# A lone tile computed with its tokens stationary and the weights moving, in a fused attention and mixture-of-experts kernel on one core

## The chip, the cores and the metric

The kernel runs on one core of a Trainium2 chip. The metric is the device time of one execution in microseconds (us), the median of the runs.

## What is computed

Per batch and head, keys and values are averaged over groups of 8, and softmax attention runs against the 72 averaged keys. The result, 4608 rows of 512, is routed: each row goes to the one of 8 experts with the largest gate, through `relu(x @ w1[e]) @ w2[e]`, and is scaled by two gate factors.

```python
x = attn_out.transpose(0, 2, 1, 3).reshape(B * S, H * D)     # 4608 x 512
e_idx = np.argmax(x @ w_gate, axis=1)
for e in range(E):
    mask = e_idx == e
    h = np.maximum(x[mask] @ w1[e], 0.0)                      # 512 -> 1024
    ye = h @ w2[e]                                            # 1024 -> 512
    out[mask] = gate_w[mask, None] * eom[mask, e, None] * ye
```

With the inputs of seed 0 the experts get 1018, 55, 333, 239, 827, 724, 24 and 1388 rows: 8, 1, 3, 2, 7, 6, 1 and 11 tiles of 128. Experts 1 and 6 have one tile each, with at most 64 rows in it: the **lone tiles**.

## The kernel before, in words

The first 180 us are attention and routing. Rows are scattered to a scratch tensor `xs`, ordered by expert; rows of a partly filled first tile stand at its end. A small table then tells every engine for each expert how many jobs of three tiles and of two tiles it has, and whether it is a lone tile (`sh.single`, L421). From there on each engine walks over the experts and their jobs by itself; semaphores order them.

Products are made in two parts for precision: every operand is split into a high part (fp32r) and a rest. Three matmuls stand for one: high x high, high x low, low x high.

A job of `size` tiles, by engine:
- TensorE, `l1` (L1056, its matmuls L1071): for 8 chunks `f` of the hidden layer, 4 pieces `d` of the input and 3 products, a 128x128 block of w1 is stationary and the tokens (128 x `size`) move, into one of three banks `p_h`. Then `l2` (L1042, L1052): per tile 24 matmuls with the hidden values stationary and 512 columns of w2 moving, into `p_y`.
- ScalarE: relu of each chunk into the high half of `ht` (L1153), the high part of the next job's tokens `xt` (L1142), and the high part of weight pieces (L1149).
- VectorE: the low half of `ht` (L1279), the turning of the next job's rows (L90), the low part of tokens (L1244) and of weight pieces (L1251), and the scaled output out of `p_y` (L1271, `y`). The last tile's output of a job is made at the head of the next job (`before`, `last_output`).
- GpSimd: row numbers and scale factors of the job (`sc`, `dst`), the gathers for later jobs, and the scatter of each tile's output (L1452), which waits for semaphore `y`.
- SyncE: loads the rows of the job after next (`load_next`), and the weights: each expert's 8 pieces (0 to 3 are w1, 4 to 7 are w2) go through 6 stage buffers of 512 KB (`stage`, L1005). A new piece is asked for when the piece six before it has been split (semaphore `wl`).

Two sets of weights lie in memory: w1a, w2a for even experts and w1b, w2b for odd ones. While expert e is worked on, its last job splits w1 of e+2 (`further`, `finish`), and its first job w2 of e+1 (`plan`).

A lone tile before: `l1` with n = 0 moves high and low tokens side by side, 256 columns, against each part of w1: 64 matmuls. VectorE adds the halves (`chunks_one`, L1297), ScalarE takes the relu, VectorE the low half; then 24 matmuls of 512 columns and one blank matmul (L1108) for the pair's empty second slot. Its weight pieces are split behind it (`behind_one`).

TensorE's experts 1 to 7 are one loop of four rounds with two experts each (`looped`), whose head is aligned to a block of instructions (`head_slot`). Each expert reads its word of the table at its start, then branches over the code of three-tile jobs if it has none; for the first expert of a round that branch carries a hint set before expert 0 (`second`, `third`), for the second it carries none.

Of the kernel before, what the change touches and what calls it, by code (L numbers as in the profile page):

```python
# [66 lines left out]
TURN_ONE = 4  # L67
FIRST = 2

# [34 lines left out]
def attention_and_routing(ctx, tc, sh, qT, kT, v, wg, wst, xs):  # L104
# [300 lines left out]
    def closing():  # L405
# [310 lines left out]
def experts(st, nc, sh, wst, xs, out):  # L716
# [14 lines left out]
    sums = sb("sums", [P, 4, P], F32)  # L731
# [7 lines left out]
    names = ["l1", "tx", "l2", "xh", "xl", "hh", "hl", "y", "sc", "c", "x0", "x1", "x2", "t", "out", "wh", "wl", "on", "ad", "g", "pre", "xs", "xu"]  # L739
# [15 lines left out]
    @contextmanager  # L755
    def jobs(eng, n, hint, few):
        if hint is None:
            with eng.If(n > 0):
                yield
            return  # L760
        name = f"jobs_{nc.next_id()}"
        some = eng.to_reg(n)
        eng.br_eq(some, 0, on_true=name + "_end", on_false=name + "_body").branch_hint(hint, few)
        with nc.body(name + "_body", valid_engines=[eng.engine]):
            yield
            eng.br(name + "_end")
        nc.switch_bb(name + "_end")

    def one_expert(eng, v, e, job, slot, body, late, far=False, hint=(None, None)):
        trips, pairs = counts(v)  # L770
        single, after_trips, after_pairs = v & 64, v & 128, v & 256
        skipped, few = hint
        if far:
            fewer = eng.alloc_register(f"few_{nc.next_id()}")
            eng.reg_mov(fewer, (pairs + 1) >> 1)
        for size, n in ((3, trips), (2, pairs)):
            with jobs(eng, n, skipped, few):
                with eng.Fori(0, n) as i:
                    if size == 3 and far:
                        skipped, few = eng.mark_branch_hint_location(), fewer  # L780
                    body(e, size, job + i, slot + i * size, single, i if size == 3 else i + trips,
                         (n - 1 - i) * 128 + after_trips if size == 3 else after_pairs - (n - 1 - i) * 256,
                         1 - (n - 1 - i) - (pairs if size == 3 else 0), late, n - 1 - i)
            job = eng.snap(job + n)
            slot = eng.snap(slot + n * size)
        return job, slot, trips, pairs, single

# [19 lines left out]
    def loops(eng, rows, body, between=None, both=None):  # L807
        job, slot, single = 0, 0, None
        at = Shared()
# [15 lines left out]
    def looped(eng, rows, body):  # L825
        third = eng.alloc_register("third")
        eng.reg_mov(third, (counts(rows[1])[0] + 15) >> 4)
        second = eng.mark_branch_hint_location()
        job, slot = one_expert(eng, rows[0], 0, 0, 0, body, None)[:2]
        job_r, slot_r = eng.alloc_register("job_r"), eng.alloc_register("slot_r")  # L830
        eng.reg_mov(job_r, job)
        eng.reg_mov(slot_r, slot)

        def whole(r, most):
            return nc.s_assert_within(eng.snap(r), 0, most, skip_runtime_bounds_check_because="there are at most 50 slots")

        with nc.Fori(0, E // 2, engines=[eng.engine], head_slot={eng.engine: 0}) as g:
            for k in range(2):
                at = nc.s_assert_within(2 * g + k, 0, E - 1, skip_runtime_bounds_check_because="experts in order")
                v = nc.values_load_multi_w_load_instructions(  # L840
                    sh.table[0:1, bass.ds(at + 1, 1)], [eng.engine], min_val=0, max_val=1023,
                    skip_runtime_bounds_check_because="counts of a few bits each")[1][0]
                job, slot = one_expert(eng, v, (at, (k + 1) % 2), whole(job_r, 50), whole(slot_r, 56), body, None, True,
                                       (None, None) if k else (second, third))[:2]
                eng.reg_mov(job_r, job)
                eng.reg_mov(slot_r, slot)
        return whole(job_r, 50), whole(slot_r, 56)

    def begin(eng, rows, names, step=None):
# [3 lines left out]
        if step is not None:  # L853
            with eng.Else():
                step(0)
                step(1)
                with eng.If((rows[E + 1] & 1) > 0):
                    step(2)

# [3 lines left out]
    def choose(eng, e, size, single, nth, many, one, split, done, late):  # L863
# [21 lines left out]
        if size == 3:  # L885
            if done is None:
                first()
            else:
                with eng.If(done <= 0):
                    first()  # L890
                with eng.Else():
                    split(plan(e, 0)[0:INIT])
        else:
# [25 lines left out]

    def behind_one(eng, e, single, split, j0, j1, late):  # L920
        rest(eng, e, 2, single, 1, split, j0, j1, None, late, None)

    def rest(eng, e, size, single, nth, split, j0, j1, done, late, left):
# [7 lines left out]
        if size == 2:  # L931
# [27 lines left out]
    def finish(eng, e, size, single, last, split, j0, j1):  # L959
        some = further(e)[j0:j1]  # L960
        if some:
            with eng.If(last - single > 0 if size == 2 else last > 0):
# [13 lines left out]
    def _(eng):  # L976
# [36 lines left out]
        def body(e, size, job, u, single, nth, more, last, late, left):  # L1013
            done = started(e, size, rows, nth)
# [3 lines left out]
            finish(eng, e, size, single, last, split, 0, 4)  # L1018
# [36 lines left out]

# [480 lines left out]
```

## Time and profile before

| | us |
|---|---|
| runs: median of 3 (lowest, highest) | 605.22 (604.93, 606.62) |
| the profiled execution, its own time | 606.98 |
| its span in the profile | 605.20 |
| expert 1's lone tile, from the end of expert 0 to the start of expert 2 | 251.54 to 266.14 |
| expert 6's lone tile | 465.50 to 478.87 |

The chain that ended last is followed back from the last instruction; its pieces say which work set the end. A piece named "issue" is time in which the engine waited for nothing that the profile shows. "x96" is the number of instructions; the time of a piece divided by it is the pitch at which they follow one another, which is shorter than the duration of one, since matmuls overlap. [...] Times on the left are counted from the span's start.

### The profile page before, as it was taken

The numbers are of one execution on the slowest core, as the hardware profiler recorded it, in microseconds if no ns is written. First come the engines' busy times: TensorE is split into PE (matmuls) and PEld (weight loads), VectorE is DVE, ScalarE is ACT, GpSimd is POOL, SyncE is SP. The second block draws the span as 40 slices with busy tenths as digits, with TensorE's granted clock in tenths as the row PEclk, the third lists the DMA queues.
The fourth block names the chain that finished last, engine by engine and source line by source line (L and its number), as shares of the span: only waits on it lengthen the run. The fifth ranks groups of instructions, "written<-read, shape, count | busy, mean of one in ns | idle before, by whom it ended". The sixth has DMA issues, their size and how long they took to land.

```text
span 605.2 us, 12486 instructions
## 1 busy us (share of the span) xinstructions
PE 577.8 (95%) x3543; PEld 529.9 (88%) x3544; DVE 354.7 (59%) x815; ACT 259.5 (43%) x693; POOL 232.2 (38%) x348
## 2 busy tenths in 40 slices
PE   1999999999989999999999999999999999999996
PEld 1899989988887989899899898999898998989895
DVE  5688889997878723599484623457154941323231
ACT  2889878897444402367262311334040520202120
POOL 3858889953535532144232122311222331212131
PEclk9999999999998999999999999999999999999999
DMA  8958889888557821748855613075223203020112
GB/s 330 350 212 310 325 304 352 334 266 235 175 158 200 269 76 36 227 132 298 265 183 192 174 46 72 18 225 145 77 54 115 62 4 86 18 69 18 52 35 70
DMA packets 49716, 99.35 MB, mean 164 GB/s; under 512 B 7070, under 2 KB 31646, under 8 KB 47840
## 3 DMA queue, kind: packets, MB, share of 16 engines
q1 hardware_dynamic: 41664, 79.24, 41.4%
q0 software_dynamic: 7968, 19.24, 8.8%
q14 instruction: 62, 0.51, 0.3%
q8 instruction: 22, 0.36, 0.3%
HBM read 77.17 MB, written 22.59 MB: 165 GB/s over the span
## 4 chain that ended last, share of the span: by engine, by line
PE 69%; issue 0%; POOL 0%; DVE 0%; POOLq 0%
PE p_h L1071 34%; PE p_y L1052 33%; PE p_y L653 2%; POOL out L1452 0%; DVE rows L1271 0%; PE p_y L1108 0%; POOLq L1419 0%; POOLq L1452 0%; POOLq L1421 0%
## 5 line engine op out<-in xcount | busy, mean ns | idle before, releaser
L1153 ACT ACTIVATE ht<-p_h 128x384 fp32r<-128x384 f32 (+1 forms) x104 | 46.8, 450 | 236.1 <-PE p_h L1071 235.9
L1452 POOL DMA_INDIRECT out<-rows,dst x41 | 43.2, 1054 | 205.5 <-DVE rows L1271 203.6
L1071 PE MATMUL p_h<-xt,w1b 128*128 128x384 f32 (+1 forms) x736 | 115.4, 317 | 1.0 <-DVE w1a L1251 1.0
L1071 PEld LDWEIGHTS p_h<-xt,w1b 128*128 128x128 f32 x736 | 114.5, 189 | 1.9 <-DVE w1a L1251 1.4
L1052 PE MATMUL p_y<-w2b,ht 128*128 128x512 f32 x480 | 110.4, 390 | 0.0
L1279 DVE SCALAR_TENSOR_TENSOR ht<-p_h,ht 128x384 fp32r<-128x384 f32 (+1 forms) x104 | 52.3, 503 | 93.3 <-ACT ht L1153 93.0
L1052 PEld LDWEIGHTS p_y<-w2b,ht 128*128 128x128 f32 x480 | 89.8, 188 | 18.4
L1052 PE MATMUL p_y<-w2a,ht 128*128 128x512 f32 x408 | 94.2, 390 | 0.4 <-PE p_y L653 0.4
L1071 PE MATMUL p_h<-xt,w1a 128*128 128x256 f32 (+1 forms) x640 | 93.3, 306 | 0.0
L1071 PEld LDWEIGHTS p_h<-xt,w1a 128*128 128x128 f32 x640 | 92.8, 190 | 0.5
L1052 PEld LDWEIGHTS p_y<-w2a,ht 128*128 128x128 f32 x408 | 76.2, 188 | 16.4 <-issue 0.9
L1271 DVE TENSOR_SCALAR rows<-p_y,sc 128x512 f32<-128x512 f32 x41 | 30.6, 750 | 101.5 <-PE p_y L1052 100.1
L282 ACT ACTIVATE p<-p_h,m 128x72 f32<-128x72 f32 x288 | 71.4, 367 | 14.5 <-DVE m L277 14.1
L299 PE MATMUL p_y<-vbd,pT 128*128 128x162 f32 (+1 forms) x480 | 73.0, 304 | 2.9 <-DVE oh L351 1.3
L299 PEld LDWEIGHTS p_y<-vbd,pT 128*128 128x128 f32 (+1 forms) x480 | 60.7, 179 | 5.4 <-ACT p L282 2.5
L1429 POOL DMA_INDIRECT xm<-xs,src x54 | 55.0, 1019 | 26.0 <-POOL src L1425 14.2
L439 POOL DMA_INDIRECT xs<-xg,where x36 | 36.8, 1022 | 31.5 <-issue 8.5
L214 POOL TENSOR_TENSOR kq<-kq 128x288 f32<-128x288 f32 (+1 forms) x63 | 40.5, 668 | 13.0 <-DMA kq<-kT 10.3
L271 PE MATMUL p_h<-kbd,q_even 128*128 128x144 f32 (+1 forms) x160 | 28.8, 307 | 12.7 <-DMA q_even<-qT 10.0
L292 ACT ACTIVATE pT<-ptr 128x384 f32<-128x384 f32 x72 | 38.5, 536 | 1.8 <-PE ptr L291 1.6
L291 PE MATMUL ptr<-ident,p 128*128 128x128 f32 x216 | 35.9, 275 | 0.9 <-DVE vbd L259 0.9
L321 DVE TENSOR_TENSOR xg<-p_y,grec 128x320 f32<-128x320 f32 x72 | 35.2, 489 | 1.5
(172 smaller groups left out, 648.1 us busy)
## 6 DMA issues: line engine op xcount, KB each, us to landing
stage<-wst SPq DMA_DIRECT2D x64, 512.0 KB, 4.9
rows<-v SPq DMA_DIRECT2D x16, 768.0 KB, 5.5
kq<-kT SPq DMA_DIRECT2D x7, 1152.0 KB, 13.6
rows<-xs SPq DMA_DIRECT2D x40, 192.0 KB, 5.8
kq<-qT SPq DMA_DIRECT2D x4, 1152.0 KB, 10.2
rows<-xs SPq DMA_DIRECT2D x64, 64.0 KB
q_even<-qT SPq DMA_DIRECT2D x3, 1152.0 KB, 10.0
xs<-stage SPq DMA_DIRECT2D x8, 257.0 KB, 9.2
```

The lines of the kernel that those rows point to most:

```text
L214: nc.gpsimd.tensor_tensor(k[:, :, 0:w], k[:, :, 0:w], k[:, :, w:2 * w], op=ALU.add)
L282: nc.scalar.activation(pt[i % 3][:, 4 * a + h, 0:KEYS], sv[:, h], AF.Exp, bias=m[:, h:h + 1])
L291: nc.tensor.transpose(tr[:, P * c:P * c + P], src[:, o:o + P], ident)
L292: nc.scalar.activation(pT_t[i][:, 3 * a:3 * a + 3, :], tr[:, 0:384].rearrange("p (c n) -> p c n", c=3), AF.Copy)
L299: nc.tensor.matmul(av[r0:r0 + n, COLS * c:COLS * c + 2 * COLS], pT[:, 3 * a + c, r0:r0 + n], vbd[b % 2][:, a, c].rearrange("p h f -> p (h ...
L439: ins = nc.gpsimd.indirect_dma_start(out=xs, out_offset=bass.IndirectOffsetOnAxis(ap=where, axis=0), in_=x.bitcast(I32), in_offset=None)
L1052: i = mm(to, ht[:, h, f, P * k:P * k + P], w[:, part, o:o + DM], start=(f == 0 and part == 0 and h == 0), stop=(f == 7 and h == 1))
L1071: i = mm(to, w[:, part, o:o + P], x, start=(d == 0 and k == 0), stop=(d == 3 and k == len(terms) - 1))
L1153: act(ht[:, 0, f, 0:n], p_h[f % 3][:, 0:n], AF.Relu).then_inc(q["hh"], 1)
L1279: nc.vector.scalar_tensor_tensor(ht[:, 1, f, 0:n], src, 0.0, ht[:, 0, f, 0:n].bitcast(F32), op0=ALU.max, op1=ALU.subtract).then_inc(q["hl" ...
L1429: nc.gpsimd.indirect_dma_start(out=xb[:, k].bitcast(I32), out_offset=None, in_=pairs_of, in_offset=bass.IndirectOffsetOnAxis(ap=src[:, k:k ...
L1452: nc.gpsimd.indirect_dma_start(out=out, out_offset=bass.IndirectOffsetOnAxis(ap=dst[:, k:k + 1], axis=0), in_=yb[2 if k == size - 1 else k ...
```

## The change

A lone tile of at most 64 rows now is a job of its own kind on TensorE. The low parts of its tokens are copied beside their high parts (`copy_low`, semaphore `lh`), so that one 128x128 block holds both; this block is stationary and w1 moves, 512 columns at a time: 16 matmuls. ScalarE copies the two sums (`flat`); TensorE multiplies each 128x128 block of them with two identities side by side (`stack`), 8 matmuls, which turns them and adds high and low rows; ScalarE takes the relu and VectorE the low part, in two pieces of four chunks; 16 matmuls of 512 columns with w2 moving follow (`l2_half`), and leave two halves in `p_y[0]`. The next job's VectorE adds them (`owing`, semaphore `fd`, two instructions). Three weight pieces are split by ScalarE amid the lone tile and two by VectorE ahead of it (`amid_one`).

TensorE's loop: no aligned head; instead its whole code behind the attention part begins at slot 41 of a block of 256 (`CODE`). The word of the next expert is read amid the expert before it. One branch at an expert's start leads to the code of a lone tile, behind that of the others; for the first expert of a round it has a hint, set in expert 0's two-tile job behind `l1`, for the second none. The branch to the two-tile jobs is hinted from the three-tile ones.

Further: expert 0 no longer treats a lone tile (`sh.single[0]` is 0); in its two-tile job VectorE finishes all four pieces of `further` ahead of the first output; SyncE holds back the four stage loads of expert 0's last job until that job's `l2` is done (`held`). The routing has two more VectorE instructions on 128x8 elements or fewer.

```diff
-        v_.tensor_scalar(sh.single, tiles, 1.0, 64.0, op0=ALU.is_equal, op1=ALU.mult)
+        v_.tensor_scalar(cnt, cnt, float(P // 2), 64.0, op0=ALU.is_le, op1=ALU.mult)
...
+        v_.memset(sh.single[:, 0:1], 0.0)
+        v_.scalar_tensor_tensor(sh.single[:, 1:E], tiles[:, 1:E], 1.0, cnt[:, 1:E], op0=ALU.is_equal, op1=ALU.mult)
...
+    def far_expert(eng, v, e, job, slot, body, amid, alone, hints, few):
...
+        start = eng.br_eq(eng.to_reg(single), 64, on_true=name + "_alone", on_false=name + "_several")
+        for h in hints:
+            start.branch_hint(h, few)
...
+            eng.br_eq(eng.to_reg(pairs), 0, on_true=name + "_end", on_false=name + "_pairs").branch_hint(skipped, paired)
...
-        with nc.Fori(0, E // 2, engines=[eng.engine], head_slot={eng.engine: 0}) as g:
+        with nc.Fori(0, E // 2, engines=[eng.engine]) as g:
...
+                at = far_expert(eng, v, (e, (k + 1) % 2), whole(eng, at[0], 50), whole(eng, at[1], 56), body,
+                                lambda: eng.reg_load(words[1 - k], sh.table[0:1, bass.ds(e + 2, 1)]), alone,
+                                [] if k else marked, few)
...
+    def amid_one(eng, e, late, split, j0, j1):
+        some = [plan(e, p)[j0:j1] for p in (0, 1)]
...
+            def held(some):
+                eng.wait_ge(q["l2"], u + size + 1)
+                split(some)
...
-            finish(eng, e, size, single, last, split, 0, 4)
+            finish(eng, e, size, single, last, split if e else held, 0, 4)
...
+        def l2_half(e, u, job):
+            w = sh.w2[parity(e)]
+            for f in range(8):
+                eng.wait_ge(q["hl"], 8 * job + f + 1)
+                o = DM * f
+                mm(p_y[0], ht[:, 0, f, 0:P], w[:, 0, o:o + DM], start=(f == 0), stop=(f == 7), skip_group_check=True)
+                i = mm(p_y[0][0:P // 2], ht[:, 0, f, P // 2:P], w[:, 1, o:o + DM], start=False, stop=(f == 7), skip_group_check=True)
+            i.then_inc(q["l2"], 2)
+
+        def one(e, u, job, amid):
+            w = sh.w1[parity(e)]
+            eng.wait_ge(q["xl"], u + 2)
+            split_by(e, 4)
+            eng.wait_ge(q["lh"], job + 1)
+            for c in range(2):
+                for d in range(4):
+                    o = FF * d + 4 * P * c
+                    for part in range(2):
+                        i = mm(p_h[c], xt[:, 0, d, 0:P], w[:, part, o:o + 4 * P], start=(d == 0 and part == 0), stop=(d == 3 and part == 1))
+                i.then_inc(q["l1"], 4)
+            amid()
+            for c in range(2):
+                eng.wait_ge(q["ad"], 8 * job + 2 + 4 * c)
+                for j in range(4):
+                    i = mm(p_h[2 - 2 * c][:, P // 2 * j:P // 2 * j + P // 2], flat[:, 4 * c + j], stack, start=True, stop=True)
+                i.then_inc(q["ad"], 2)
+            eng.wait_ge(q["y"], u + 2)
+            split_by(e, 8)
+            l2_half(e, u, job)
...
+        eng.addr_align(256, offset=CODE, max_nops=0)
         eng.nop().then_inc(q["l2"], 1)
...
-        def chunks_one(job):
-            for f in range(8):
-                eng.wait_ge(q["ad"], 8 * job + f + 1)
-                act(ht[:, 0, f, 0:P], sums[:, f % 4], AF.Relu).then_inc(q["hh"], 1)
+        def chunks_one(job, behind):
+            for c in range(2):
+                behind(c)
+                eng.wait_ge(q["l1"], 8 * job + 4 * c + 4)
+                act(flat[:, 4 * c:4 * c + 4], p_h[c].rearrange("p (j n) -> p j n", j=4), AF.Copy).then_inc(q["ad"], 2)
+            for c in range(2):
+                eng.wait_ge(q["ad"], 8 * job + 6 + 2 * c)
+                act(ht[:, 0, 4 * c:4 * c + 4, P // 2:P], turned_one(c), AF.Relu).then_inc(q["hh"], 4)
...
+                eng.wait_ge(q["l2"], u + 1)
+                chunks_one(job, lambda c: amid_one(eng, e, late, split, 2 * c, 2 + c))
...
+        def owing(u, job):
+            low, high = slice(0, P // 2), slice(P // 2, P)
+            with eng.If(whole(eng, at.owed, 2) - 1 > 0):
+                eng.wait_ge(q["l2"], u + 1)
+                eng.wait_ge(q["sc"], job)
+                nc.vector.tensor_scalar(fold[high], p_y[0][low], sc[high, 0:1], None, op0=ALU.mult).then_inc(q["fd"], 1)
+                eng.wait_ge(q["fd"], job + 1)
+                nc.vector.scalar_tensor_tensor(yb[0][high], p_y[0][high], sc[high, 0:1], fold[high],
+                                               op0=ALU.mult, op1=ALU.add).then_inc(q["y"], 1)
...
+        def chunks_one(job, more, u, begin):
+            begin()
+            eng.wait_ge(q["xl"], u + 2)
+            for c in range(2):
+                tx(c, job + 1)
+                eng.wait_ge(q["hh"], 8 * job + 4 * c + 4)
+                nc.vector.scalar_tensor_tensor(ht[:, 0, 4 * c:4 * c + 4, 0:P // 2], turned_one(c), 0.0,
+                                               ht[:, 0, 4 * c:4 * c + 4, P // 2:P].bitcast(F32),
+                                               op0=ALU.max, op1=ALU.subtract).then_inc(q["hl"], 4)
+            with eng.If(more > 0):
+                eng.wait_ge(q["y"], u + 2)
+                tx(2, job + 1)
...
+                chunks_one(job, more, u, lambda: amid_one(eng, e, late, split, 0, 2))
```

## Rows read from the trace of the kernel before

**Rows 1.** The page, busy time of each engine.
```profile
PE 577.8 (95%) x3543; PEld 529.9 (88%) x3544; DVE 354.7 (59%) x815; ACT 259.5 (43%) x693; POOL 232.2 (38%) x348
```
**Rows 2.** The chain that ended last: start us, us, what.
```profile
251.54 0.98 issue
252.52 7.93 PE p_h L1071 x64
260.44 5.47 PE p_y L1052 x24
265.91 0.23 PE p_y L1108
266.14 16.66 PE p_h L1071 x96
...
465.50 7.67 PE p_h L1071 x64
473.18 5.47 PE p_y L1052 x24
478.64 0.23 PE p_y L1108
```
**Rows 3.** ACT, groups by line and shape: busy us, mean ns.
```profile
L1153 ACT ACTIVATE ht<-p_h 128x256 fp32r<-128x256 f32 x40 | 15.3, 383 | 103.6 <-PE p_h L1071 103.4
L1149 ACT ACTIVATE w2a<-stage 128x1024 fp32r<-128x1024 f32 x12 | 12.3, 1058 | 0.2 <-issue 0.2
L1142 ACT ACTIVATE xt<-p_y 128x512 fp32r<-128x512 f32 x7 | 4.2, 599 | 8.4 <-DVE p_y L90 8.4
```
**Rows 4.** DVE, groups by line and shape.
```profile
L1271 DVE TENSOR_SCALAR rows<-p_y,sc 128x512 f32<-128x512 f32 x41 | 30.6, 750 | 101.5 <-PE p_y L1052 100.1 <-issue 1.3
L90 DVE STREAM_TRANSPOSE p_x<-rows 128x512 f32<-128x512 f32 x32 | 21.0, 701 | 0.0
L1244 DVE TENSOR_TENSOR xt<-p_x,xt 128x512 fp32r<-128x512 f32 x32 | 20.6, 684 | 0.8 <-ACT xt L1142 0.4
L1279 DVE SCALAR_TENSOR_TENSOR ht<-p_h,ht 128x256 fp32r<-128x256 f32 x40 | 16.8, 421 | 30.4 <-ACT ht L1153 30.4
L1251 DVE TENSOR_TENSOR w2a<-stage,w2a 128x1024 fp32r<-128x1024 f32 x12 | 14.4, 1218 | 1.7 <-ACT w2a L1149 1.6
```
**Rows 5.** Timeline of PE, 80 to 86 us: the smallest f32 matmuls at full pitch.
```profile
80.77 0.49 PE L291 MATMUL ptr<-ident,p 128*128 128x128 f32 x3
81.10 0.99 PE L299 MATMUL p_y<-vbd,pT 128*128 128x162 f32 x6
```
**Rows 6.** SP's transfers, 196 to 300 us, and the stage transfers of 246 to 266 us.
```profile
248.14 3.73 SPq L1005 DMA_DIRECT2D stage<-wst  x4
...
DMA to landing us min/median/max: 4.2/5.1/6.3
```
**Rows 7.** Timeline of ACT and DVE, 222 to 310 us.
```profile
241.90 3.91 ACT L1149 ACTIVATE w1a<-stage 128x1024 fp32r<-128x1024 f32 x4
...
246.90 4.62 DVE L1251 TENSOR_TENSOR w1a<-stage,w1a 128x1024 fp32r<-128x1024 f32 x4
251.58 0.75 DVE L1271 TENSOR_SCALAR rows<-p_y,sc 128x512 f32<-128x512 f32 x1
```
**Rows 8.** Stretches: PE busy, PEld, DVE, ACT, POOL, granted clock, DMA share, GB/s.
```profile
178.00:180.50 2.50, 0.69 (x4) 0.22 (x2) 0.00 (x0) 0.00 (x0) 0.06 (x1) 1.00 0.01 3
...
181.50:182.50 1.00, 1.00 (x4) 0.82 (x3) 0.96 (x3) 0.82 (x1) 0.99 (x1) 0.50 0.03 8
...
184.50:186.00 1.50, 1.50 (x8) 1.22 (x7) 0.73 (x4) 0.00 (x0) 0.49 (x1) 0.94 1.23 223
...
252.50:253.50 1.00, 0.98 (x8) 0.99 (x9) 0.00 (x0) 0.00 (x0) 0.28 (x1) 1.00 1.02 414
```
**Rows 9.** Timeline of PE and of POOL, at the end of the attention part.
```profile
180.54 9.36 PE L653 MATMUL p_y<-w2a,ht 128*128 128x512 f32 x33 [1.85 <-PEq L1508]
...
171.37 0.97 POOL L399 DMA_INDIRECT xs<-kbd,tail_at  x1 [0.30 <-DVE rows L673]
```

More of the change, by code (lines that the diff above doesn't have):

```diff
@@ L753, in counts, with one_expert @@
         return trips, pairs
[L755 to L769, printed above, removed]
+    def one_expert(eng, v, e, job, slot, body, late):
         trips, pairs = counts(v)
         single, after_trips, after_pairs = v & 64, v & 128, v & 256
[L772 to L775, printed above, removed]
         for size, n in ((3, trips), (2, pairs)):
-            with jobs(eng, n, skipped, few):
+            with eng.If(n > 0):
                 with eng.Fori(0, n) as i:
[L779 to L783, printed above, removed]
+                    each(e, size, i, n, job, slot, body, trips, pairs, single, after_trips, after_pairs, late)
             job = eng.snap(job + n)
@@ L823, in loops, with looped @@
         return job, slot
[L825 to L828, printed above, removed]
+    def looped(eng, rows, body, alone, marked):
+        few = eng.alloc_register("few")
+        eng.reg_mov(few, 1 - ((rows[1] >> 6) & 1))
         job, slot = one_expert(eng, rows[0], 0, 0, 0, body, None)[:2]
[L830 to L835, printed above, removed]
-        with nc.Fori(0, E // 2, engines=[eng.engine], head_slot={eng.engine: 0}) as g:
-            for k in range(2):
[L839 to L847, printed above, removed]
@@ L961, in finish @@
         if some:
-            with eng.If(last - single > 0 if size == 2 else last > 0):
+            with eng.If(last - single > 0 if size == 2 and e else last > 0):
                 split(some)
@@ L1081, in body @@
             else:
-                with eng.If(single > 0):
-                    l1(e, size, u, job, 0)
-                with eng.Else():
-                    l1(e, size, u, job, size * P)
-            eng.wait_ge(q["y"], u + 1)
+                two(e, u, job, more)
+                return
+            eng.wait_ge(q["y"], u + 2)
             if done is not None:
@@ L1127, in _ @@
         begin(eng, rows, [("l1", 8)])
-        job, slot = looped(eng, rows, body)
+        job, slot = looped(eng, rows, body, one, marked)
         eng.wait_ge(q["xl"], slot + 2)
@@ L1323, in many, with behind @@
                 more = begun(s, nth)
-                chunks(job, s, lambda f: between_chunks(eng, e, f, nth, late, split, s == 2))
+                def behind(f):
+                    if f == 0:
+                        owing(u, job)
+                        eng.reg_mov(at.owed, 1)
+                    between_chunks(eng, e, f, nth, late, split, s == 2)
+                chunks(job, s, behind)
                 after(s, more, True)
@@ L1344, in hidden @@
                 chunks(job, size, lambda f: split(some[f:f + 1]))
-            def hidden_one(some):
-                chunks_one(job, more)
-            before(job, u)
+            before(u)
             done = started(e, size, rows, nth)
@@ L1407, in _ @@
         assert ticks[0] == ROWS
-        last_output(loops(eng, rows, body, between, both)[1])
+        job, u = loops(eng, rows, body, between, both, at)
+        before(u)
+        owing(u, job)
     @blk.gpsimd
```

209 lines of the change are left out of this document (139 added, 70 removed).

## The prediction

> **What bounds the kernel now.** I read the page first: TensorE is busy for 95% of the span, the next engine for 59% [rows 1]. Then the chain that ended last. From 251 us on it is TensorE piece after piece, and the reader should look for what is not TensorE in it: one piece "issue", 0.98 us in front of expert 1's lone tile [rows 2]. So the end moves by what TensorE's own stream loses or gains, plus any new wait in it. A lone tile now costs TensorE 7.93 + 5.47 + 0.23 = 13.63 us for expert 1 (14.60 with the 0.98, 251.54 to 266.14) and 7.67 + 5.47 + 0.23 = 13.37 us for expert 6 [rows 2]. Both are plain streaming: 64 matmuls of 256 columns at 0.120 us, 24 of 512 columns at 0.228 us. Last I read the groups of ScalarE and VectorE, because the new lone tile is so short that their steps will order it.
>
> **TensorE's own work in the new lone tile.** 16 + 16 matmuls of 512 columns at 0.228 [rows 2] are 3.65 + 3.65 us. The 8 turning matmuls are f32 with 64 columns; the trace has none of that kind. The nearest are 128x128 f32 ones, three in 0.33 us, 0.11 each [rows 5]; half of that is the floor, a 162-column one, 0.99 / 6 = 0.165, the ceiling. I take 0.11: 0.9 us. That is 8.2 us against 13.4; the rest is waiting.
>
> **The chain of expert 6's lone tile**, counted from its first matmul. TensorE: first half of the sums 1.9, second half 3.8. ScalarE meanwhile splits two weight pieces (a run of four takes 3.91 us, 0.98 each [rows 7]): 0.1 to 2.1; copies the first half, 0.60 (the nearest is its 128x512 copy [rows 3]): 2.7; splits a third piece, 1.06 [rows 3]: 3.75, just in time for the second copy, 3.8 to 4.4. TensorE turns the first four blocks 3.65 to 4.1 and the second four 4.45 to 4.9. ScalarE's relu of 128x256, 0.38 [rows 3]: 4.4 to 4.8 and 5.1 to 5.5. VectorE's low half, 0.42 [rows 4]: 4.85 to 5.3; one turning of rows, 0.65 to 0.70 [rows 4], to 5.95; second low half, to 6.4. The last matmuls: 5.3 to 7.1 and 7.1 to 9.0. So 9.0 us in place of 13.4: **-4.4 us**. VectorE's remaining list in that time, the third turning (7.0), ScalarE's copy of it (0.60, 7.65) and three low parts of 0.68 [rows 4] from 7.05, ends at about 9.0 as well: the next expert's tokens are just in time. Its total (one output 0.75, two pieces of 1.16, three turnings, three low parts, two low halves) is 8.0 of 9.0 us. There is no room left, so any delay on VectorE now shows.
>
> **Expert 1's lone tile** has one wait more. ScalarE's third piece there is (expert 2, piece 6), and its load is one of the four that SyncE now holds until expert 0's last matmul. Before, these four went out from 248.14 to 251.87, each behind a split [rows 6, 7]. Now they go out at +0.35 us and the first lands 4.2 to 6.3 us later, the span of those four transfers [rows 6]. I take 4.2, since nothing is in front of it: 4.55. ScalarE splits it to 5.6 and copies the second half to 6.2; the second turning ends at 6.7, the relus at 6.6 and 7.3, the low halves at 7.1 and 8.2, the matmuls at 8.9 and 10.8. VectorE's tokens for expert 2 are ready at 10.75. So 10.8 us. TensorE stands still from 4.1 to 6.25 in it.
>
> **The branch into expert 1.** The 0.98 us is put down to a split of w1a, but that one had ended at 251.52 (246.90 + 4.62 [rows 7]), and the chain calls it issue: the engine was getting at its code, past an aligned loop head and a jump, while transfers filled 1.02 of the DMA engines [rows 8]. After the change there is one jump, with a hint set 11 us earlier, the table's word is there already, and `held` keeps the four stage loads out of that time. I take 0, bounds 0 and 1.85 (the longest wait of TensorE's sequencer in these rows [rows 9]). Expert 1 then goes from 14.60 to 10.8: **-3.8 us**.
>
> **The rest, costed at nothing.** Expert 6's branch and the way back to the loop's head have no hint, as in the kernel before: there expert 6 came over the unhinted jump without a gap, 64 matmuls in 7.67 us being full pitch [rows 2]; 1.85 us each is the upper bound. Cover is the queue of matmuls in front, now 1.8 us (eight of 512 columns) in place of 5.5. `owing` adds two VectorE instructions of up to 0.75 us [rows 4] at the next job's first chunk; TensorE looks at that chunk's low half only at its fifth chunk, over 6 us later (16.66 / 8 = 2.1 us each [rows 2]). GpSimd's scatter of the lone tile waits for it, some 13 us later than the scatter of a job's first tile would, and the next scale factors queue behind that; they are wanted after 16.7 + 5.5 us of the next job [rows 2], some 17 us after the scatters may start, and a scatter takes GpSimd about 1 us [rows 9] with its landing behind. `copy_low` and `stack` lie in the jobs before. Finishing expert 0's four pieces ahead of its first output delays only that output. The two routing instructions (under 0.2 us each, of the size of its neighbours) come before the scatter at 171.37, TensorE's barrier wait starts at 178.7 when its own work is done [rows 9]: nothing, at most 0.3. The jump over the padding at slot 41 falls into that wait; if the code is not there, up to 1.85 us.
>
> **Sum.** 4.4 + 3.8 = 8.2 us. Against the profiled execution's 606.98 (span 605.20 and 1.78 around it) that is 598.8. That execution lies 1.76 above the median of the runs, so for the median I take the difference: 605.22 - 8.2 = **597.0 us**.
>
> [...]
>
> **Rivals and chances.**
> - Forecast, both chains as above, no fall of the clock: 596.2 to 597.8. Chance 0.42.
> - The clock falls in expert 1 (for: a longer stand than 1.85; against: TensorE works for 0.45 us in the middle of it), or piece 6 lands at 6.3 instead of 4.2 (2.1 us later): 598.6 to 599.1, both 600.7. Chance 0.30.
> - Piece 6 lands in time (SyncE's four loads no longer wait for splits), expert 1 takes 9.0: 595.2. Chance 0.10.
> - Code is late at one or two of the jumps without a hint or at the padding: 0.98 to 1.85 each, 598 to 600.7. For: only 1.8 us of matmuls now cover them. Against: expert 6's jump cost nothing before, and the chain has no "issue" of more than the 0.98 behind 200 us until the end, so neither did the ways back. Chance 0.11. [...]
> - Slower: without the aligned head the loop's blocks no longer fall where they did, and each of the six starts of experts 2 to 7 pays a code wait. It decides from 1.4 us each on (8.2 / 6); at the 1.85 of [rows 9] it is 11.1 - 8.2 = 2.9 us slower, 608.1. Against: those starts are preceded by 5.5 us of queued matmuls. Chance 0.03.
> - The lone path does what it says, but VectorE's and ScalarE's lists run longer than their rows (semaphore turns, branches), and the next expert's tokens come 3 us late in both: 603, about no change. Chance 0.04.
>
> A difference under 0.3% (1.8 us) can't be told from none. Faster by more is all but the last two: 0.92; same 0.05, slower 0.03. The range for 8 in 10 takes in the early piece at its floor, 595.2 less 0.6 for cheaper turnings (8 x 0.055 and two shorter waits), and both the clock and a late piece: 594.6 to 600.7.
>
> **What would show it.** In the chain, expert 1's three pieces should shrink to about 10.8 us and expert 6's to 9.0, with no "issue" in front of expert 1; matmuls of 128x512 out of `p_h` 16 per lone tile at 0.228. ScalarE should be seen waiting for a stage transfer in expert 1 and not in expert 6. PEclk should be 1.00 in 250 to 270 us. Expert 2's and expert 7's first chunks should follow at once. Wrong would be: "issue" pieces at starts of experts, a granted clock of 0.50 in expert 1, or an equal lone tile in both experts.

## The result, and the profile after

The changed kernel took 611.34 us, median of 4 runs (611.0 to 611.85), beside 605.23 us before (4 runs, 604.93 to 606.62): a ratio of 1.0097, 95% interval 1.0079 to 1.0115. It is slower by about 6 us, where 8.2 us less had been forecast. The profiled execution took 611.85 us, its span is 610.1 us, 4.9 more than before.

The page of the changed kernel, busy time of each engine and the granted clock of TensorE by slices of the span (PEclk, in tenths of full speed):

```profile
PE 575.9 (94%) x3461; PEld 525.6 (86%) x3462; DVE 347.4 (57%) x792; ACT 259.3 (42%) x685; POOL 234.0 (38%) x348
PEclk9999999999898999989989999999999999999999
```

TensorE does less work than before in fewer instructions (577.8 with 3543 in [rows 1]), and the span is longer: the loss is standing time, and time at a lower clock. Of the four slices with an 8, the third (259 to 275 us) and the fourth (305 to 320 us) lie behind stands that the change brought. The first (152 to 168 us) lies in the attention part, and the second (183 to 198 us) has an 8 before the change too.

The chain that ended last, of the changed kernel (start us, us, what):

```profile
230.68 11.51 PE p_h L1135 x96
242.19 10.92 PE p_y L1089 x48
253.13 3.62 DMA stage<-wst
...
260.57 0.41 DVE ht L1377
261.03 0.50 PE p_y L1098
...
262.04 0.43 PE p_y L1099
...
266.55 16.66 PE p_h L1135 x96
283.21 16.36 PE p_y L1089 x72
299.57 5.99 issue
305.56 13.53 PE p_h L1135 x96
...
473.96 0.06 DVE rows L1351
...
479.31 0.41 DVE ht L1377
479.76 0.50 PE p_y L1098
...
483.74 16.67 PE p_h L1135 x96
```

Set this beside [rows 2], stretch by stretch:

| | before | after | difference |
|---|---|---|---|
| end of expert 0 | 251.54 | 253.13 | +1.6 |
| expert 1's lone tile | 14.60 | 13.42 | -1.2 |
| start of expert 3, with its first `l1` | 11.5 | 5.99 + 13.53 | +8.0 |
| expert 6's lone tile | 13.37 | 9.78 | -3.6 |

The sum is +4.8 of the 4.9 between the spans. For expert 3 the chain of the kernel before has no piece between the `l2` ahead of it and its `l1`:

```profile
282.80 16.36 PE p_y L1052 x72
299.17 11.51 PE p_h L1071 x96
```

Two readings matter. The one large new piece is "issue", 5.99 us, in front of expert 3, a plain two-tile job that the change was not about. And the `l1` behind it takes 13.53 us where 96 matmuls of the same shape take 11.51 in expert 0 (230.68). The stretches of the changed kernel around it say what TensorE did (columns as in [rows 8]):

```profile
262.00:263.00 1.00, 1.00 (x4) 0.70 (x3) 1.00 (x2) 0.67 (x2) 0.00 (x0) 0.50 0.00 0
299.50:305.50 6.00, 0.07 (x1) 0.00 (x0) 0.75 (x1) 0.00 (x0) 0.98 (x1) 0.77 0.42 152
305.50:306.50 1.00, 0.94 (x4) 0.94 (x5) 0.00 (x0) 0.00 (x0) 0.10 (x1) 0.50 0.03 8
306.50:308.50 2.00, 2.00 (x12) 2.00 (x11) 0.00 (x0) 0.00 (x0) 0.53 (x4) 0.50 0.00 0
```

From 299.5 to 305.5 nearly every engine is idle; then the granted clock is 0.50 for 3 us and more. That is the 2 us on top of the wait. The first line is the second fall, in expert 1. What the 6 us were spent on shows in the transfers of queue q8, one of two queues that bring instructions. The profile does not say for which engine. I take its blocks for TensorE's, since in all the kernels below one of them starts within 1.5 us of the start of each "issue" of TensorE over 1 us behind the attention part. That queue's line in the transfers of the changed kernel (packets of 16 KB, MB, share), first for 244 to 256 us, then 256 to 296, then 296 to 306:

```profile
q8 instruction: 2, 0.03, 1.3%
...
q8 instruction: 2, 0.03, 0.3%
...
q8 instruction: 3, 0.05, 2.8%
```

In half-microsecond windows the last three start at 299.5, 300.5 and 304.5, one after another while TensorE stands. By this reading expert 3 waited for code. How the 6 us divide among the blocks is not shown: the third starts some 1 us before TensorE goes on, and in x2_code_169 below, with a gap of the same length, only two start in it (300.96 and 301.75).

### The profile page after: what moved, and what is told of

It reads as the page before. It is cut to its first block, busy times and chain, and to the rows that moved or that the text cites. A ratio compares the mean times of both kernels' runs of the same rounds, so it can differ in the third digit from the quotient of the medians.

```text
span 610.1 us, 12455 instructions
## 1 busy us (share of the span) xinstructions
PE 575.9 (94%) x3461; PEld 525.6 (86%) x3462; DVE 347.4 (57%) x792; ACT 259.3 (42%) x685; POOL 234.0 (38%) x348
## 4 chain that ended last, share of the span: by engine, by line
PE 66%; issue 2%; DMA 1%; DVE 1%; DVEq 0%; ACT 0%; POOL 0%; POOLq 0%; ACTq 0%
PE p_h L1135 32%; PE p_y L1089 31%; PE p_y L655 2%; PE p_y L1098 1%; PE p_y L1099 1%; DMA stage<-wst 1%; DVE w2b L1316 0%; PE p_h L1117 0%; POOL out L1570 0%; DVE rows L1351 0%; DVE ht L1377 0%; ACT flat L1222 0%; ACT ht L1225 0%; DVEq L815 0%; DVEq L1304 0%
## 5 line engine op out<-in xcount | busy, mean ns | idle before, releaser
L1135 PE MATMUL p_h<-xt,w1b 128*128 128x384 f32 (+1 forms) x672 | 109.4, 324 | 6.0 <-issue 6.0
L1135 PEld LDWEIGHTS p_h<-xt,w1b 128*128 128x128 f32 x672 | 108.5, 193 | 6.9 <-issue 6.4
L1089 PE MATMUL p_y<-w2b,ht 128*128 128x512 f32 x456 | 104.8, 390 | 0.0
L1089 PEld LDWEIGHTS p_y<-w2b,ht 128*128 128x128 f32 x456 | 85.4, 188 | 17.4
L1089 PE MATMUL p_y<-w2a,ht 128*128 128x512 f32 x384 | 88.5, 390 | 0.4 <-PE p_y L655 0.4
L1135 PE MATMUL p_h<-xt,w1a 128*128 128x384 f32 (+1 forms) x576 | 85.5, 309 | 0.0
L1135 PEld LDWEIGHTS p_h<-xt,w1a 128*128 128x128 f32 x576 | 85.0, 190 | 0.5
L1089 PEld LDWEIGHTS p_y<-w2a,ht 128*128 128x128 f32 x384 | 71.8, 188 | 15.5 <-issue 0.9
L1351 DVE TENSOR_SCALAR rows<-p_y,sc 128x512 f32<-128x512 f32 x37 | 27.7, 750 | 100.6 <-PE p_y L1089 98.5
L1547 POOL DMA_INDIRECT xm<-xs,src x54 | 57.0, 1056 | 26.1 <-POOL src L1543 14.2
L214 POOL TENSOR_TENSOR kq<-kq 128x288 f32<-128x288 f32 (+1 forms) x63 | 40.6, 671 | 12.8 <-DMA kq<-kT 12.2
```

What stands on the lines that cost most here:

```text
L214: nc.gpsimd.tensor_tensor(k[:, :, 0:w], k[:, :, 0:w], k[:, :, w:2 * w], op=ALU.add)
L1089: i = mm(to, ht[:, h, f, P * k:P * k + P], w[:, part, o:o + DM], start=(f == 0 and part == 0 and h == 0), stop=(f == 7 and h == 1))
L1135: i = mm(to, w[:, part, o:o + P], x, start=(d == 0 and k == 0), stop=(d == 3 and k == len(terms) - 1))
L1547: nc.gpsimd.indirect_dma_start(out=xb[:, k].bitcast(I32), out_offset=None, in_=pairs_of, in_offset=bass.IndirectOffsetOnAxis(ap=src[:, k:k ...
```

## The experiments

"Gap" below is the "issue" piece in front of expert 3 in the chain (5.99 us in the changed kernel). Edits are against the changed kernel. The time from the end of expert 0 to the end of the span, 353.7 us before and 357.0 after, compares them without the attention part, whose length differs between executions.

**Is it the code's place?** The aligned loop head was put back, or the code was moved by half a block.

```diff
-        with nc.Fori(0, E // 2, engines=[eng.engine]) as g:
+        with nc.Fori(0, E // 2, engines=[eng.engine], head_slot={eng.engine: 0}) as g:
...
-        eng.addr_align(256, offset=CODE, max_nops=0)
```

> The changed kernel with TensorE's alignment as before: the loop over the experts begins at slot 0 of a block of instructions, its code ahead of it is not aligned. In the changed kernel TensorE waits 5.99 us for code at expert 3's start, the first way back to the loop's head, and runs 2.0 us longer at the low clock behind it. Theory A (the new place of the code in its blocks): the 5.99 us fall to under 1, the time to about 603.3. Theory B (expert 1 now jumps past the code of several tiles, so expert 3 is the first to need it, wherever it lies): 5 to 7 us stay, about 611.

Ratio 1.0079 (1.004 to 1.0118), median 610.41 us. The chain of this kernel:

```profile
296.01 6.04 issue
302.05 14.41 PE p_h L1135 x96
```

The aligned head makes no difference to the gap. The same with `CODE = 169` in place of 41:

> The changed kernel with TensorE's code at slot 169 of a block in place of 41, all else as it is. Theory A (place in the blocks): the wait at expert 3's start changes by over 2 us. Theory B (code needed for the first time): it stays at 5 to 7 us.

612.9 us in one run, a gap of 6.03 us, and 2.06 us of "issue" at 189.6, in expert 0, where the changed kernel has 0.43. At the three places tried, small waits moved about, and the gap did not.

**Is it the way back to the loop's head?** Expert 3 is the first of the loop's second round. A hint was put on the way back (`hint_back_edge=True` in the `Fori`).

> The changed kernel with a hint for the loop's closing branch at the top of each round. If the missing code is the loop's head, the wait of 5.99 us at expert 3 falls by 2 us or more. If it is the code that expert 1 jumped past, behind the head, it stays within 1 us.

610.76 us, gap 6.07: no help. Whether the second hint did anything beside the first, no run here shows.

**Does the gap belong to expert 1's path?** Expert 1 was run as a two-tile job, everything else as in the changed kernel.

```diff
-        v_.memset(sh.single[:, 0:1], 0.0)
-        v_.scalar_tensor_tensor(sh.single[:, 1:E], tiles[:, 1:E], 1.0, cnt[:, 1:E], op0=ALU.is_equal, op1=ALU.mult)
+        v_.memset(sh.single[:, 0:2], 0.0)
+        v_.scalar_tensor_tensor(sh.single[:, 2:E], tiles[:, 2:E], 1.0, cnt[:, 2:E], op0=ALU.is_equal, op1=ALU.mult)
```

> The changed kernel with expert 1 told as not a lone tile, so that it runs as a job of two tiles through the same code that expert 3 will need; expert 6 stays lone. Expert 1 takes 11.5 + 10.9 = 22.4 us in place of 13.4, 9 more. Theory B (code needed for the first time): the wait at expert 3's start is under 1 us and the first chunks there run at full clock; the time is 611.3 + 9 - 8, about 612, and a wait of several us stands in front of expert 1 if no hint brings that code. Theory A (place in the blocks): the wait at expert 3 stays 5 to 7 us, the time is about 620.

612.75 us, with expert 1 at 22.4 us. In front of expert 3 its chain has:

```profile
307.89 0.36 issue
308.25 11.77 PE p_h L1135 x96
```

The way back and the branches of expert 3 are the same, and they cost 0.36 us; the `l1` behind them takes 11.77 us, within 0.3 of the 11.51 in expert 0, and does not lose the 2.0 us either. So neither the way back nor expert 3's own branches cost 6 us in themselves: the gap depends on what expert 1 did, on how it was entered or on which code it ran.

**Would one more hint help?** In the lone path, a hint was set for the branch over the three-tile jobs.

```diff
+            over = eng.br_eq(eng.to_reg(trips), 0, on_true=name + "_amid", on_false=name + "_trips")
...
+            over.branch_hint(eng.mark_branch_hint_location())
```

> The changed kernel with one more hint: in the lone path, ahead of its first matmul, for the branch of the same expert's code that jumps over the three-tile jobs (expert 3 takes it next). Theory B1 (one jump whose target was never fetched costs the 5.99 us): the wait at expert 3's start falls under 1 us and with it the low clock behind it, 2.0 us; the time is about 611.3 - 8.0 = 603.3. Theory B2 (several fetches in a row, of the loop's head and of two later blocks): 2 us or more of the wait stay, the time is 605 or more.

Ratio 1.0087 (1.0054 to 1.012), gap 6.97 us. It did not help.

**Is it the table's word?** TensorE's read of the next expert's word was moved ahead of the three-tile jobs (`amid()` called earlier).

> The changed kernel with the next expert's word read ahead of the three-tile jobs in place of behind them. Theory E (TensorE's sequencer can't run ahead of the last matmuls because the read stands between them and the jump, so the whole wait for code shows): the wait at expert 3 falls by 2 us or more. Theory F (the wait is longer than any lead the queue gives, or the queue gives none): it stays within 1 us of 6.0.

615.23 us in one run, gap 5.03 and 14.23 us of `l1` behind it: still there, though 1 us shorter. That is theory F.

**Is it the hint into expert 1's lone path?** That hint was taken away, and nothing else.

```diff
-                                [] if k else marked, few)
+                                [], few)
```

> The changed kernel without the hint for the branch to expert 1's lone path. If a jump to code that was never fetched costs what expert 3 showed, 5 to 7 us of issue stand in front of expert 1 and the time is 5 to 9 us longer, 616 to 620. If the queued matmuls cover it, nothing changes.

606.43 us, span 604.7. Its chain:

```profile
244.09 10.92 PE p_y L1089 x48
...
301.70 0.23 issue
301.93 11.77 PE p_h L1135 x96
```

The gap is gone, 0.23 us, and the `l1` behind it takes 11.77. From the end of expert 0 (255.01) to the end it is 349.7 us, 7.3 less than the 357.0. The wait that I expected in front of expert 1 in its place was a miss: TensorE stood 0.30 us there.

```profile
255.29 3.01 PE L1111 MATMUL p_h<-w1b,xt 128*128 128x512 f32 x12 [0.30 <-issue]
```

Timed again:

> The changed kernel without the hint into expert 1's lone path, timed. If the hint alone is what expert 3 pays for, the profile shows no wait over 0.5 us at expert 3 and at most 0.5 us in front of expert 1, and the time is 611.3 - 8.0 + 0.3 = 603.6. If the one look before was chance, 609 to 612.

606.8 us, ratio 0.9977 (0.9944 to 1.001), 0.45 us in front of expert 3 and 0.34 in front of expert 1. The kernel before ran at 607.79 us beside it, 2.6 more than at first, so the ratio is what can be compared with the forecast: 0.9977 x 605.2 = 603.8, where 603.6 was expected. In the transfers of x8_no_hint1, queue q8 has, for 246 to 256 us and for 296 to 306 us:

```profile
q8 instruction: 3, 0.05, 2.1%
...
q8 instruction: 1, 0.02, 0.6%
```

One block more around the start of expert 1 (249.0, 252.5 and 255.5; in the changed kernel 247.0 and 250.5), and one in place of three at expert 3, which starts at 302.2, when its `l1` already runs. So without the hint two blocks come before the end of expert 0 (255.01) and the third as expert 1's first matmuls run, and expert 3 waits for none. That the third is code that expert 3 needs is argued from this, not shown; which block it is, and why the hint leaves it out, the traces do not say. One more rival stands untested: the hint is set once, in expert 0, for a branch that expert 3 takes too, the other way, and no run shows whether it still acts there. What the runs do show is that the hint makes the gap. In the nine profiles with it and a lone expert 1 the gap is 5.0 to 7.0 us, in the five without it (this kernel twice, and the three further down) 0.23 to 0.45.

**What holds expert 1 up?** It took 13.42 us where 10.8 had been forecast. SyncE's held loads were set free:

```diff
-            finish(eng, e, size, single, last, split if e else held, 0, 4)
+            finish(eng, e, size, single, last, split, 0, 4)
```

> The changed kernel without the hold on SyncE: the four stage loads of expert 0's last job go out as its pieces are split. If the held load sets expert 1 (ScalarE waits 3.6 us for it from expert 1's start), its lone tile falls from 13.4 to about 9 to 11 us, and the low clock in it goes. If VectorE's own late start sets it (its first split piece comes 3.8 us after its output, for no wait that the profile shows), it stays within 0.7 us of 13.4. If the hold is there to keep code from coming late, an issue of 1 us or more stands in front of expert 1.

609.77 us in one run; expert 1 from 252.14 to 264.36, 12.2 us, between the two figures expected, so the hold cost 1.2. The low clock stayed (last matmuls at 0.43 us), and nothing stood in front of expert 1, as long as the hint was there. Then VectorE's two pieces ahead of the low hidden half were put behind the lone tile instead (hold and hint as in the changed kernel):

```diff
-                chunks_one(job, more, u, lambda: amid_one(eng, e, late, split, 0, 2))
+                chunks_one(job, more, u, lambda: None)
...
-            behind_one(eng, e, single, split, 2, 4, late)
+            behind_one(eng, e, single, split, 0, 4, late)
```

> The changed kernel with VectorE's two weight pieces behind the lone tile in place of ahead of its turnings. If these 2.4 us of VectorE set the lone tile, expert 6 falls from 9.8 to about 7.5 us and expert 1 from 13.4 to 11 or less. If what sets it is VectorE's sequencer (3.5 us from its output to its next instruction in expert 6), expert 6 falls by under 1 us.

610.77 us in one run, the gap still there (6.10). Expert 1 took 10.2 us (254.2 to 264.45) with its last matmuls at 0.23 us each, so the clock did not fall in it. Expert 6 took 9.52, not the 7.5 expected: all of it is now TensorE's own work. But expert 2's `l1` now took 17.3 us in place of 16.7, with 0.85 us of VectorE's "issue" in the chain: VectorE came late with its low half.

**All three together**, no hint, no hold, VectorE's pieces behind:

> Three undone together in the changed kernel: the hint into expert 1's lone path, SyncE's hold, and VectorE's two weight pieces ahead of the lone tile (now behind it). Theory C (the three act in different places and add up): no wait at expert 3 (-8.0), expert 1's lone tile about 9.6 us in place of 13.4 (no wait for a held load, no VectorE list, no low clock), expert 6's 9.5, expert 2's first layer 0.6 longer: 611.3 - 11.5 = 599.8, faster than both kernels. Theory D (without the hold, code comes late in front of expert 1 since there is no hint): 1 to 3 us of issue there, 601 to 603.

605.57 us, ratio 0.9984 (0.9956 to 1.0012), not told from no change, though from the end of expert 0 (255.12) to the end it is 348.7 us, 5.0 less than before. The three do not simply add up: theory D came true beside theory C, and TensorE stood 2.37 us in front of expert 1.

```profile
257.49 0.73 PE L1111 MATMUL p_h<-w1b,xt 128*128 128x512 f32 x2 [2.37 <-issue]
```

This is what the hold had been good for. Without the hint, TensorE stands 0.30 and 0.34 us there with the hold (the two profiles above) and 2.37, 1.38 and 2.40 without it (this kernel and the next two). In all five, expert 1's first matmul comes 2.8 us behind the start of a block of q8. With the hold that block starts 2.4 to 2.5 us before expert 0 ends, without it 0.4 to 1.4. Taking the hold alone away, as in x5_no_held, does the same: there the second block of q8 around expert 1's start comes 5.9 us behind the first, in the changed kernel 3.4. Why it comes later is not shown; the four stage loads are on their way just then. A kernel without the hint, with the hold and with VectorE's pieces behind was not run.

With one of VectorE's pieces put back amid the lone tile:

> As the kernel with three undone, but VectorE splits one weight piece between its first and second turning of rows, where it waited 2.8 us for ScalarE. If that gap holds it, expert 2's first layer loses its 0.6 us and the lone tiles stay at 9.5: 599.2. If the piece delays the first low half, expert 6 grows by up to 1.2 us: 600 to 602.

606.26 us, ratio 0.9991 (0.9961 to 1.002), and the same 0.85 us of VectorE in the chain in expert 2, whose `l1` is about 0.3 us shorter than in z1_three, half of the 0.6 expected. VectorE's timeline of z1_three at that place names what stands between the first two chunks (idle before in brackets):

```profile
271.27 0.55 DVE L1359 SCALAR_TENSOR_TENSOR ht<-p_h,ht 128x384 fp32r<-128x384 f32 x1
271.85 0.75 DVE L1341 TENSOR_SCALAR flat<-p_y,sc 64x512 f32<-64x512 f32 x1
272.63 0.76 DVE L1343 SCALAR_TENSOR_TENSOR rows<-p_y,sc,flat 64x512 f32<-64x512 f32 x1
274.10 1.23 DVE L1316 TENSOR_TENSOR w1b<-stage,w1b 128x1024 fp32r<-128x1024 f32 x1 [0.71 <-DVEq L1346]
275.36 0.56 DVE L1359 SCALAR_TENSOR_TENSOR ht<-p_h,ht 128x384 fp32r<-128x384 f32 x1
```

The low half of chunk 0 comes at 271.27, that of chunk 1 only at 275.36: the lone tile's output made in the next job, `owing`, and a weight piece lie between them. So `owing` was moved behind the fourth chunk, on top of the three edits, and the kernels before and after were run beside it on the same chip.

```diff
-                    if f == 0:
+                    if f == 3:
                         owing(u, job)
```

> As z1_three (no hint into expert 1's lone path, no held load, VectorE's pieces behind the lone tile), and the deferred output of the lone tile made behind the fourth chunk of the next job in place of the first. What took 1.31 us of VectorE plus 0.71 us of its sequencer between chunks 0 and 1 of expert 2 goes to where VectorE is ahead, so expert 2's l1 takes 16.7 to 17.0 us from first to last matmul in place of 17.49. From expert 1's start to the end 345.5 to 346.5 us. Chip theory: the ratio is 0.980 to 0.987. Change theory, where it starts expert 1 some 2 to 5 us later than before: 0.988 to 0.995.

602.72 us, ratio **0.9942 (0.9917 to 0.9967)**: this one is faster than the kernel before by 0.6%, and so than the changed one. Its chain:

```profile
250.89 2.40 issue
253.29 3.92 PE p_h L1111 x16
...
263.10 16.72 PE p_h L1135 x96
279.82 16.36 PE p_y L1089 x72
296.18 0.23 issue
296.41 11.77 PE p_h L1135 x96
...
463.01 3.63 PE p_h L1111 x16
466.64 0.85 PE p_h L1117 x8
...
467.54 1.10 PE p_h L1117 x8
...
472.49 16.64 PE p_h L1135 x96
```

Expert 2's `l1` is back at 16.72 us, expert 6 takes 9.48, all of it TensorE's work, and an "issue" of 2.40 us stands in front of expert 1. From the end of expert 0 (250.89) to the end it is 347.9 us, 5.5 less than in the kernel before on the same chip (353.4, below). The ratio lies in the band that I had set for a changed kernel that starts expert 1 later than before (0.988 to 0.995), not in the other.

> The kernel before, looked at again beside the two below on one chip. Chip theory: what lies ahead of expert 1 (its l1 began at 251.54 us in the first profile of before, between 252 and 258 us in those of the changed kernel) differs by the chip, so here before begins expert 1 within 0.5 us of the changed kernel. Change theory: the changed program is itself 1.5 us or more later there (its start at L653 was 180.5 before, 181 to 185 in eleven profiles after), so before stays 1.5 us or more ahead on this chip too. From the start of expert 1 to the end 353.7 us by both, within 1 us.

> The changed kernel again. Both theories: the 6 us gap and the 2 us at the lower clock in front of expert 3 come again, and from expert 1's start to the end it takes 357.0 us within 1 us. Chip theory: expert 1 starts as late as in before on this chip, and the ratio is 1.0055 (3.3 of 605). Change theory: it starts 1.5 us later, and the ratio is 1.008 to 1.010.

The kernel before: one run of 604.85 us, span 603.1, end of expert 0 at 249.67. The changed kernel: 612.41 us, ratio 1.0099 (1.0069 to 1.013), span 609.5, end of expert 0 at 251.77. Its chain and, in it, the gap came again:

```profile
251.77 3.82 DMA stage<-wst
...
298.75 5.94 issue
304.69 13.82 PE p_h L1135 x96
```

From the end of expert 0 to the end that is 353.4 us before and 357.7 after. Up to the end of expert 0 the changed program was 2.1 us later than the kernel before on one chip, and v_owing 1.2 us. In the trace of v_after two places show: the matmuls behind the attention part go on at 181.66 (L655) in place of 180.26, and expert 0's first `l1` has a wait of 0.38 us for VectorE's low half. The first need not be the change: TensorE's wait in front of it is as long as before (1.47 and 1.42 us), so 1.35 of the 2.1 us lie ahead of that wait, in TensorE's attention part, whose code is the same. From 120 to 160 us the granted clock was 0.96 there, and 1.00 in v_before and in v_owing, whose wait starts within 0.1 us of v_before's. What is left, 0.7 us in v_after and 1.2 in v_owing, is on one chip, so it speaks for the change, by one profile of each.

## Why the prediction was wrong

**The step that failed** is in "The branch into expert 1" and "The rest, costed at nothing". "After the change there is one jump, with a hint set 11 us earlier ... I take 0": at that jump this was right, there is no "issue" in front of expert 1 but 0.02 us (253.12). That the 0.98 us there before were TensorE getting at its code was my reading, which the transfers do not show: in the trace of before blocks of q8 start in the half microseconds from 248.5 and 254.0, and none between. But I priced the hint only where it points. Taking it away alone removes the gap at expert 3 and the fall of the clock behind it: 5.99 + 13.53 us become 0.23 + 11.77, 7.5 less, nearly the whole saving that I had forecast. Behind it stands a second error: the ways back and unhinted jumps "cost nothing before", so I took them as free. That they were free said nothing about the new program, which has other code at other places and enters expert 1 by another way. With the hint, expert 3 paid where it had not paid before. Why the hint does this stays open.

**"Cover is the queue of matmuls in front"** fell with it. In front of expert 3 stood an `l2` of 72 matmuls, 16.36 us, and covered nothing: the first of the three fetches starts in the half microsecond from 299.5, in which that `l2` ends (299.57). From this I take it that TensorE's sequencer reached the branch hardly earlier than its last matmul ended. In front of expert 1 in x8_no_hint1 the block starts 2.5 us before the queue ends; there the queue covered all but 0.30 us. Expert 6's jump, free in [rows 2], had spoken for cover. But in the trace of before no block of q8 starts after 365.57, so nothing was being brought when that jump came at 465.50, and that it was free shows nothing of what a jump costs whose code is still to come.

**The rivals.** "Code is late at one or two of the jumps without a hint" came nearest, with late code at 0.11, priced at 0.98 to 1.85 us each from [rows 9]; measured 5.99 plus 2.0 at the low clock. It looked for the cause in the jumps without a hint, and the run without any hint into expert 1 has no such wait. My slower rival blamed the missing aligned head; x1_loop_head, with the head back, has the same 6.04. It got the sign by the wrong part. The clock rival came true as well: in expert 1 the last matmuls follow at 0.43 us in place of 0.23 (262.04 in the chain).

**Expert 1: -3.8 forecast, -1.2 measured.** The lone tile took 13.42 us in place of 10.8. The stage load landed 3.62 us after expert 1's start, better than my 4.55, in which 0.35 for its going out was an estimate without a row. The first low half ended 7.9 us after the start (260.98 - 253.13), where I had 7.1, and the 16 last matmuls took 5.52 us (261.03 to 266.55), where I had 3.7. So about 0.8 us is VectorE's side and 1.8 the clock, which fell in them. The forecast put the fall at nothing, and the clock rival at 1.6 (598.6 in place of 597.0). No run shows that term: the runs showed 1.8 us here and 2.0 in expert 3's `l1`. In the trace of before the granted clock was 0.50 from 181.5 to 184.5 us, behind the wait of 1.85 us in [rows 9]. Here it fell without so long a stand: not one of 2.2 us, but two of 0.79 and 1.55. VectorE's timeline in the changed kernel:

```profile
253.14 0.75 DVE L1351 TENSOR_SCALAR rows<-p_y,sc 128x512 f32<-128x512 f32 x1 [2.89 <-PE p_y L1089]
257.67 2.36 DVE L1316 TENSOR_TENSOR w2a<-stage,w2a 128x1024 fp32r<-128x1024 f32 x2 [3.78 <-issue]
259.94 0.72 DVE L90 STREAM_TRANSPOSE p_x<-rows 128x512 f32<-128x512 f32 x1
260.57 0.40 DVE L1377 SCALAR_TENSOR_TENSOR ht<-p_h,ht 128x256 fp32r<-128x256 f32 x1
```

Between its output and its weight pieces VectorE idles 3.78 us, waiting for nothing that the profile shows; my list had no such term. The pieces, 2.36 us, then lie ahead of the low half that TensorE waits for. In x6_dve_behind, with the pieces out of the way, the clock did not fall and expert 1 took 10.2. Whether the 3.78 us are the sequencer's own steps or VectorE's code coming late no run tests: in expert 6 the same place takes 1.70, and in the 3.78 us a block of the second queue of instructions, q14, starts (255.8).

**Expert 6: -4.4 forecast, -3.6 measured.** Same mechanism, two sizes off: 9.78 in place of 9.0. In the changed kernel the chain runs over VectorE: the first low half ended 5.8 us after the start (479.72 - 473.96), where I had 5.3, and the 16 last matmuls took 4.0 us in place of 3.7. With VectorE's pieces behind, TensorE's own work alone is 9.52, since the turnings are longer than I took: 0.85 + 1.10 = 1.95 us in v_owing's chain, where I had 0.9. That one was to be read: I wrote that the trace has no f32 matmul of 64 columns, but the group of `vg` (L256) in the trace of before is 128x128 by 128x64 f32, 48 records in 6.3 us, 0.13 each. The new turnings show two records for each matmul, 16 per lone tile, so this row gives 2.1 us.

**Ahead of expert 1: at most 0.3 and, if code is late at the padding, 1.85 forecast; 1.6 and 2.1 measured** in the two profiles of the changed kernel. Of these, 1.5 and 1.35 us lie in TensorE's attention part, where the granted clock fell in both (0.96 from 120 to 160 us, 1.00 in the two profiles of before). One more block of q8 starts behind the padding than before, but after TensorE has gone on (182.35 against 181.66 in v_after), so it is not what that start waited for. The medians say more: with the difference from the end of expert 0 on taken off, 6.1 - 3.3 and 6.9 - 4.3, the changed kernel comes 2.8 and 2.6 us later to expert 1. This is an estimate, from medians and one profile each. The forecast's 0.3 is too small by that; what the time goes to, no run shows.

**`owing`, costed at nothing**, is nothing in the changed kernel, but expert 2's `l1` is 0.6 us longer (17.3 in place of 16.7) as soon as VectorE's pieces are put behind the lone tile. The cover that I named, four chunks of slack, holds only while VectorE is not behind.

What was right: that the lone tile's own work shrinks, though less than forecast (8.2 us). With the three disturbances away, it takes 9.48 us in expert 6 and 9.81 in expert 1 behind its "issue" of 2.40 us (253.29 to 263.10), against 13.37 and 13.63 before.

## What to carry to other kernels

A branch hint can move a wait instead of removing it (here nothing in front of expert 1 and 5.99 us in front of expert 3 with it, 0.30 and 0.23 without): look at the instruction queue's transfers over the next experts or rounds, not only at the branch it is for, and try the kernel without it. Do not count on queued matmuls to cover a branch (16.36 us of them covered nothing of the 5.99): look in the trace when the fetch starts and when the last of them ends. What one edit costs or saves can hang on another: the hold cost 1.2 us with the hint, and without the hint it kept a wait of 1 to 2 us away. When a step is shortened on one engine, add the time that the engines that feed it stand between two instructions, and put whatever can wait behind the operand that is waited for.

## What had not been expected

- A hint that left no wait at the branch it was for cost 5.99 us, and 2.0 us of low clock, some 45 us later; without it that branch cost 0.30 us.
- Behind the 6 us stand the granted clock was 0.50 for over 3 us. In expert 1 of x5_no_held the clock fell too (last matmuls at 0.43 us), in x6_dve_behind, with a single wait of 0.81 us, it did not.
- VectorE idled 3.78 us between its output and the next instruction, waiting for nothing that the profile shows, in the middle of a job of 13 us.
- Holding back four loads, which looked like a pure loss of 1.2 us, kept 1 to 2 us of "issue" away from expert 1 once the hint was gone (0.30 and 0.34 with the hold, 1.38 to 2.40 without).
- The code's place by half a block moved a wait of 2.06 us into expert 0 (0.43 before the move).
